# New durations in the table from which a kernel's planner orders every engine: an RWKV scan and two feed-forward layers on one Trainium2 core

## The chip, the core and the metric

The kernel runs on one core of a Trainium2 chip. The core has five engines with an instruction queue each: TensorE (PE, matmuls), VectorE (DVE), ScalarE (ACT), GpSimd (POOL) and SyncE (SP, which here issues all transfers from and to HBM). The metric is the device time of one launch in microseconds (us), lower is better; "the time" is the median of several runs.

## What is computed

Cut to what matters, the reference is:

```python
for t in range(S):                                  # 4 batches, 8 heads, 768 steps, width 48
    cur = einsum('bhd,bhe->bhde', u * kt, vt)
    y[:, :, t] = einsum('bhd,bhde->bhe', rt, state + cur)
    state = wt[..., None] * state + einsum('bhd,bhe->bhde', kt, vt)
x = y as (3072 tokens, 384)
h = x @ w_in;  x = (max(h, 0) + alpha * min(h, 0)) @ w_out      # 384 -> 2048 -> 384
h = x @ w_in2; out = (h * clip(h + 3, 0, 6) / 6) @ w_out2
```

The inputs and the result are float32.

## The kernel before

**Attention units.** The scan is cut into 48 units, each a quarter of the heads (two heads, 112 partitions) over 256 steps. Four units with the same steps are a third. A unit n loads its k, r and decays (`un`, 337 KB), runs two scans of the decays on DVE (lines 386 and 402, into `tg`), multiplies k and r by them (`kr`, line 423, DVE or POOL), and then goes through PE three times: scores and a transpose (`A`, lines 477 and 484), the state update (`kv`, lines 516 and 520, after ACT copied `kT`), and the output (`y`, lines 588 to 599). In between DVE puts the masked scores into `X` (lines 494 and 499) and updates `Y`, and ACT builds the diagonal `X` (458) and the states `sbd` (538). The result of a unit is split into a high part (ACT, 635) and a rest (DVE, 641). For units 0, 1 and 2 of a third these go straight into `xt`, the input of the first layer; for unit 3 they go into `x3`, which six small transfers (line 651) spread over `xt`. Each third also needs two loads of 128 tokens (`rk`, 384 KB), two multiplications of each (line 332, DVE or POOL) and a sum (`p`, line 339), and one load of v.

**Layers.** A layer runs 6 token blocks of 512 tokens by 16 slices of the hidden width: 96 slots, 192 in both layers. A slot is nine matmuls of 128x512 for `h` and nine for the three accumulators `acc` (three passes each, high and low parts), and between them `q` (ACT), `pg` (DVE, 808 or 812), `g` high (ACT, 818) and `g` low (DVE or POOL, 821). Slot s has `h`s, `q`s, `pg`s, `g`s. Before a slice is used for the first time, its two weights (384 KB each, `wraw`) are decoded: line 95 on ACT, lines 98 and 103 on DVE, 738 on ACT, 742 on DVE or POOL. `wraw0_f_0` is the first layer's weight of slice f into h, `wraw0_f_1` the one out of it.

**What sets the order.** The class `Plan` simulates the five engines with a list of operations, each with the engines that may run it, a duration for each of them in us, and a due time. At each step it takes the engine that can start soonest, and on it the ready operation with the earliest due time; an operation that DVE or POOL may run goes to whichever takes it first. Operations marked `pair` on DVE and all of POOL never overlap in this simulation. The sequence that comes out is the order in which every engine's instructions are written; at run time each engine works through its own list in that order, waiting where an input is not there. Fillers (line 682, `warm`, matmuls of 128x256 with no use for the result) are put on PE wherever the simulation finds it free before the first slot, and dropped after. A load on SP is planned with 1.12 us for 384 KB (1.0 for a unit) plus 2 us:

```python
            d = o["where"][e] * (2 if e == "PE" and t < self.COLD else 1)
            o["eng"], o["start"], o["end"] = e, t, t + d
            ...
            if e == "SP":
                o["end"] = t + d + 2.0
```

A load also waits for its buffer: there are three for `un`, two for `rk` and two for v. A weight of the first layer has a place of its own, so its load waits for nothing but its turn on SP.

Of the kernel before, what the change touches and what calls it, by code (L numbers as in the profile page):

```python
# [229 lines left out]
def fast_path(es, tc, unit, tok, vch, ub, w1, w2, alpha, out, flag, alp, x2d):  # L230
# [11 lines left out]
    plan = Plan()  # L242
# [50 lines left out]
    o_alpha = plan.op({"SP": 0.5}, -20.0, lambda e: nc.sync.dma_start(alp, alpha))  # L293
# [8 lines left out]
    Ylast, Yop = {}, {}  # L302
# [8 lines left out]
    def add_third(t):  # L311
# [9 lines left out]
        reds = []  # L321
        for c in range(2):
# [28 lines left out]
            reds.append(plan.op({"DVE": 0.47}, due + 4.5 + c, red, [o], new=[pb], use=[rb]))  # L351
        p_op[t] = reds, pb

    def add_unit(n):
# [46 lines left out]
        def scan_g(e):  # L401
# [8 lines left out]
        gb = plan.buf("gfirst", 2)  # L410
        o_t = plan.op({"DVE": 0.34}, d - 3.7, scan_t, [o_load], new=[tgb], use=[ub_], pair=True)
        o_f = plan.op({"DVE": 0.07}, d - 2.4, floor, [o_t], use=[tgb])
        o_d1 = plan.op({"DVE": 0.08}, d - 2, recip, [o_f], new=[gb])
        o_g = plan.op(
            {"DVE": 0.34}, d - 1.5, scan_g, [o_d1], use=[tgb, ub_, gb], pair=True
        )
# [12 lines left out]
        if early:  # L429
            o_kr = [  # L430
                plan.op(
                    {"DVE": 0.35, "POOL": 0.69}, d - 1, lambda e, i=i: scaled(e, slice(i, i + 1)),
                    [(o_t, o_g)[i]], new=[krb], use=[ub_, tgb], pair=True,
                )
                for i in range(2)
            ]
# [22 lines left out]

        o_x = plan.op({"ACT": 1.18}, d - 1, diag, reds, new=[xb], use=[pb])  # L460

# [66 lines left out]
        else:  # L528
            o_kv = plan.op({"PE": 0.1 + 0.13 * nkv}, d + 0.4, kv, kv_after, use=kv_use)
        o_tri = plan.op({"DVE": 0.61}, d - 1.5, triangle, [o_kv, o_x], use=abufs + [xb])  # L530

# [72 lines left out]
        def add_output(due=d + 2, more=0.0, then=None, after=(), use=()):  # L604
# [38 lines left out]
            fresh = [xt_buf[j]] + ([x3b] if x3b else [])  # L643
            o_hi = plan.op({"ACT": 0.36}, d + 2.5, hi_, [o_pc], new=fresh, use=[yb2])
            o_lo = plan.op({"DVE": 0.35}, d + 2.5, lo_, [o_hi], new=fresh, use=[yb2])
            ops += [o_hi, o_lo]
# [43 lines left out]
    def add_range(key, due, after=None, use=(), raw=None, behind=()):  # L690
# [78 lines left out]
    def add_slot(m, j, f):  # L769
# [9 lines left out]
        def h_(e):  # L779
# [44 lines left out]

        o_q = plan.op({"ACT": 0.58}, s + 1.1, pq, [o_h, o_alpha], new=[qb], use=[hb])
        o_g = plan.op({"DVE": 0.62}, s + 0.8, gate, [o_q], new=[pb], use=[qb, hb])
        o_1 = plan.op({"ACT": 0.52}, s + 1.0, ghi, [o_g], new=[gb], use=[pb])
        o_2 = plan.op({"POOL": 1.23, "DVE": 0.61}, s + 1.2, glo, [o_1], use=[pb, gb], pair=True)

# [366 lines left out]
```

## Time and profile before

| | us |
|---|---|
| time, median of 3 runs (944.39 to 947.23) | 945.42 |
| the profiled execution, its time | 945.74 |
| the profiled execution, its span | 944.0 |
| PE busy (share of the span) | 920.3 (97%) |
| DVE busy | 556.3 (59%) |
| ACT busy | 530.9 (56%) |
| POOL busy | 132.3 (14%) |

The span is the time from the first to the last instruction in one profiled execution; its own time is 1.7 us longer. Busy time is the time in which at least one instruction of the engine ran. The average over the whole span mixes a start, in which attention units and weights are prepared, with a long stretch in which only the slots and their units run.

### The profile page before, as it was taken

The page shows a single profiled execution, that of the slowest core. Times are in us where ns is not written, and L with a number is a line of the kernel's source. Part 1 is how long each engine was busy: PE and PEld are TensorE (multiplying, and loading weights), DVE is VectorE, ACT ScalarE, POOL GpSimd, SP SyncE. Part 2 cuts the span into 40 slices and gives each one's busy share as a digit, 9 for nine tenths or more (in the row PEclk, how much of TensorE's full clock was granted, in tenths as well). Part 3 has the DMA queues.
Part 4 walks back from the last instruction along what each step waited for, and adds up shares of the span by engine and source line. Part 5 has one row for each costly group of instructions (what it writes and reads, how often), then busy time and mean ns, then how long its engine had stood idle before and what let it go on. Part 6 is the DMA issues. An engine that isn't in the chain of part 4 may idle for free.

```text
span 944.0 us, 13745 instructions
## 1 busy us (share of the span) xinstructions
PE 920.3 (97%) x4914; PEld 743.2 (79%) x4914; DVE 556.3 (59%) x1087; ACT 530.9 (56%) x1266; POOL 132.3 (14%) x132
## 2 busy tenths in 40 slices
PE   7899989999999999999999999999999999999996
PEld 5677767878888788878888888888888888888885
DVE  8999997465655645564369886353353443443432
ACT  5998776565656655665378876363353453443331
POOL 4333234021121201100011130000000000000000
PEclk9999999999999999999999999999999999999998
DMA  8888214122312310110056530060140320500001
GB/s 250 256 268 283 81 52 145 55 79 70 107 64 57 109 55 31 58 64 7 9 186 197 175 111 1 1 200 1 54 147 1 123 79 1 172 30 1 34 1 38
DMA packets 36750, 86.20 MB, mean 91 GB/s; under 512 B 5056, under 2 KB 7488, under 8 KB 36672
## 3 DMA queue, kind: packets, MB, share of 16 engines
q1 hardware_dynamic: 36672, 85.22, 28.8%
q8 instruction: 41, 0.67, 0.3%
q14 instruction: 37, 0.30, 0.1%
HBM read 73.41 MB, written 9.44 MB: 88 GB/s over the span
## 4 chain that ended last, share of the span: by engine, by line
PE 82%; DVE 1%; DMA 0%; POOL 0%; issue 0%; POOLq 0%; DVEq 0%
PE acc L765 13%; PE acc L767 13%; PE acc L766 13%; PE h L765 12%; PE h L767 12%; PE h L766 12%; PE A L477 2%; PE y L595 1%; PE y L588 1%; PE A L484 1%; DMA rk<-in_tok 0%; PE y L599 0%; PE A L516 0%; POOL rk L332 0%; PE A L520 0%; DVE rk L332 0%
## 5 line engine op out<-in xcount | busy, mean ns | idle before, releaser
L765 PE MATMUL acc<-g,w 128*128 128x512 f32 x576 | 228.9, 397 | 0.0
L767 PE MATMUL acc<-g,w 128*128 128x512 f32 x576 | 224.6, 390 | 0.0
L766 PE MATMUL acc<-g,w 128*128 128x512 f32 x576 | 224.5, 390 | 0.0
L818 ACT ACTIVATE g<-pg 128x512 fp32r<-128x512 f32 x192 | 120.6, 628 | 137.7 <-PE acc L767 126.8
L821 DVE TENSOR_TENSOR g<-pg,g 128x512 fp32r<-128x512 f32 x176 | 121.7, 691 | 124.8 <-ACT g L818 124.7
L765 PEld LDWEIGHTS acc<-g,w 128*128 128x128 f32 x576 | 108.1, 188 | 23.4 <-issue 0.4
L767 PEld LDWEIGHTS acc<-g,w 128*128 128x128 f32 x576 | 108.1, 188 | 22.8
L766 PEld LDWEIGHTS acc<-g,w 128*128 128x128 f32 x576 | 108.2, 188 | 21.6 <-DVE g L821 0.3
L812 DVE SCALAR_TENSOR_TENSOR pg<-q,h 128x512 f32<-128x512 f32 x96 | 65.9, 686 | 98.6 <-ACT q L803 98.4
L808 DVE SCALAR_TENSOR_TENSOR pg<-h,q 128x512 f32<-128x512 f32 x96 | 66.1, 688 | 96.4 <-ACT q L801 96.3
L803 ACT ACTIVATE q<-h,three 128x512 f32<-128x512 f32 x96 | 65.8, 685 | 100.5 <-PE h L767 100.3
L765 PE MATMUL h<-xt,w 128*128 128x512 f32 x288 | 116.3, 404 | 1.2 <-ACT w L738 1.1
L767 PE MATMUL h<-xt,w 128*128 128x512 f32 x288 | 113.0, 392 | 0.9 <-POOL w L742 0.7
L766 PE MATMUL h<-xt,w 128*128 128x512 f32 x288 | 112.3, 390 | 0.0
L765 PE MATMUL h<-x,w 128*128 128x512 f32 x288 | 112.0, 389 | 0.0
L766 PE MATMUL h<-x,w 128*128 128x512 f32 x288 | 112.0, 389 | 0.0
L767 PE MATMUL h<-x,w 128*128 128x512 f32 x288 | 112.0, 389 | 0.0
L801 ACT ACTIVATE q<-h,nal 128x512 f32<-128x512 f32 x96 | 65.6, 684 | 73.6 <-PE h L767 71.7
L423 POOL TENSOR_TENSOR kr<-un,tg 112x512 f32<-112x512 f32 (+1 forms) x43 | 43.6, 1016 | 225.5 <-PE y L588 207.3
L765 PEld LDWEIGHTS h<-xt,w 128*128 128x128 f32 x288 | 54.9, 191 | 13.3 <-ACT w L738 2.2
L767 PEld LDWEIGHTS h<-xt,w 128*128 128x128 f32 x288 | 54.0, 188 | 14.1 <-DVE w L742 1.4
L766 PEld LDWEIGHTS h<-x,w 128*128 128x128 f32 x288 | 54.1, 188 | 11.3
(93 smaller groups left out, 1262.7 us busy)
## 6 DMA issues: line engine op xcount, KB each, us to landing
wraw<-in_w SPq DMA_DIRECT2D x64, 384.0 KB, 3.7
un<-in_unit SPq DMA_DIRECT2D x48, 337.3 KB, 3.2
raw<-in_w SPq DMA_DIRECT2D x32, 384.0 KB, 3.9
rk<-in_tok SPq DMA_DIRECT2D x24, 384.0 KB, 4.0
v<-in_vch SPq DMA_DIRECT2D x12, 384.0 KB, 3.1
x2d<-st SPq DMA_DIRECT2D x18, 256.0 KB, 2.1
x2r<-x2d SPq DMA_DIRECT2D x18, 256.0 KB, 4.6
out<-st SPq DMA_DIRECT2D x18, 256.0 KB, 3.5
```

The source lines that it names most:

```text
L423: eng[e].tensor_tensor(out=u["kr"][:, i].rearrange("p a (c s) -> p a c s", c=2), in0=u["in"][:, 0 : 2 * TH].rearrange("p (a c s) -> p a c ...
L477: nc.tensor.matmul(A[h][:, cs], kr[r0 : r0 + D, 0, cs], kr[r0 : r0 + D, 1, cs], start=True, stop=True,)
L484: nc.tensor.transpose(T[:, c, :], kr[:, 0, c * C : (c + 1) * C], ident[0:PR, 0:PR])
L765: nc.tensor.matmul(ps, whi, xhi, start=start, stop=False, skip_group_check=True)
L766: nc.tensor.matmul(ps, whi, xlo, start=False, stop=False, skip_group_check=True)
L767: nc.tensor.matmul(ps, wlo, xhi, start=False, stop=stop, skip_group_check=True)
L801: nc.scalar.activation(q, k["h"], AF.Relu, scale=nal[:, f : f + 1])
L803: nc.scalar.activation(q, k["h"], AF.Relu, bias=three)
L808: nc.vector.scalar_tensor_tensor(out=p, in0=k["h"], scalar=0.0, in1=k["q"], op0=ALU.max, op1=ALU.subtract)
L812: nc.vector.scalar_tensor_tensor(out=p, in0=k["q"], scalar=6.0, in1=k["h"], op0=ALU.min, op1=ALU.mult)
L818: nc.scalar.activation(k["g"][:, 0], k["p"], AF.Copy)
L821: eng[e].tensor_tensor(out=k["g"][:, 1], in0=k["p"], in1=k["g"][:, 0].bitcast(F32), op=ALU.subtract)
```

## The change

Most of the durations that the planner's list gives to operations on PE, DVE, ACT and POOL are replaced. Nearly all grow: on DVE the scans go from 0.34 to 0.69 each, a 384-wide operation from 0.47 to 0.55, `pg` from 0.62 to 0.69; on ACT the diagonal from 1.18 to 1.56, the states from 0.45 to 0.66, `g` high from 0.52 to 0.63; on PE `h` from 1.945 to 2.04 and an accumulator's three matmuls from 0.648 to 0.68. On POOL `rk` and the weights' low part go from 0.96 to 1.06 and 1.05, `g` low from 1.23 to 1.33, and `kr` of 112x512 from 1.25 down to 1.08. The loads' durations, the due times and everything else stay. No instruction is computed differently; what moves is the order on each engine, and the choice between DVE and POOL. A few lines of the diff:

```diff
-                    {"POOL": 0.96, "DVE": 0.47}, due + 2 + c, lambda e, b=b, m=mul: m(e, b=b),
+                    {"POOL": 1.06, "DVE": 0.55}, due + 2 + c, lambda e, b=b, m=mul: m(e, b=b),
...
-        o_t = plan.op({"DVE": 0.34}, d - 3.7, scan_t, [o_load], new=[tgb], use=[ub_], pair=True)
+        o_t = plan.op({"DVE": 0.69}, d - 3.7, scan_t, [o_load], new=[tgb], use=[ub_], pair=True)
...
-                    {"DVE": 0.61, "POOL": 1.25}, d - 1, lambda e: scaled(e, slice(0, 2)), [o_g],
+                    {"DVE": 0.7, "POOL": 1.08}, d - 1, lambda e: scaled(e, slice(0, 2)), [o_g],
```

What the new order holds, counted: PE has 206 fillers instead of 128, all ahead of the first slot. Up to the low part of the last weight of the first layer POOL has 57 instructions of the plan instead of 43 (`rk` 18 for 11, `kr` of 112x512 10 for 3, `kr` of 112x256 8 for 11, weights 13 for 10, `g` 7 and 7, one other). Up to `pg16` DVE has 3 `rk`, 7 `kr` of 112x512 and 3 weight operations (742) fewer, and 3 `kr` of 112x256 and 2 sums (339) more. From slot 20 on, PE's order differs only in where a unit's `A` stands between the three accumulators of a slot.

Three places, before and after. In the rows the number right behind a name is that of the unit, the load or the weight (`un6`, `rk7`, `wraw0_2_0`); the last number only tells buffers apart.

SP before, from unit 5's load to unit 7's, issued some 17 to 26 us into the span:

```order
L368 DMA un5_324<-in_unit 112x771
L729 DMA wraw0_1_0_343<-in_w1 128x384
L368 DMA un6_366<-in_unit 112x771
L328 DMA rk4_386<-in_tok 128x768
L729 DMA wraw0_2_0_409<-in_w1 128x384
L328 DMA rk5_429<-in_tok 128x768
L368 DMA un7_459<-in_unit 112x771
```

SP after the change, from unit 5's load to `rk4`:

```order
L368 DMA un5_321<-in_unit 112x771
L729 DMA wraw0_2_0_339<-in_w1 128x384
L729 DMA wraw0_0_1_366<-in_w1 128x384
L729 DMA wraw0_3_0_377<-in_w1 128x384
L729 DMA wraw0_1_1_399<-in_w1 128x384
L729 DMA wraw0_4_0_418<-in_w1 128x384
L368 DMA un6_439<-in_unit 112x771
L328 DMA rk4_458<-in_tok 128x768
```

Five weights stand between units 5 and 6 where one stood (`wraw0_1_0` comes ahead of `un5` now).

SP before, from `rk6` to the six transfers of `x3` of the second third (one row for all six), which the first slot needs:

```order
L328 DMA rk6_670<-in_tok 128x768
L729 DMA wraw0_4_0_688<-in_w1 128x384
L368 DMA un11_709<-in_unit 112x771
L729 DMA wraw0_2_1_731<-in_w1 128x384
L328 DMA rk7_745<-in_tok 128x768
L368 DMA un12_767<-in_unit 112x771
L651 DMA xt0_294<-x3_1_749 16x2x256 x6
```

SP after the change, the same stretch:

```order
L328 DMA rk6_633<-in_tok 128x768
L729 DMA wraw0_5_0_651<-in_w1 128x384
L729 DMA wraw0_3_1_676<-in_w1 128x384
L729 DMA wraw0_6_0_687<-in_w1 128x384
L368 DMA un10_706<-in_unit 112x771
L729 DMA wraw0_4_1_730<-in_w1 128x384
L328 DMA rk7_744<-in_tok 128x768
L729 DMA wraw0_7_0_762<-in_w1 128x384
L368 DMA un11_784<-in_unit 112x771
L729 DMA wraw0_5_1_800<-in_w1 128x384
L317 DMA v3_813<-in_vch 128x768
L729 DMA wraw0_8_0_832<-in_w1 128x384
L651 DMA xt0_334<-x3_1_825 16x2x256 x6
```

Between `rk6` and `rk7` stand four weights instead of two, and five loads instead of one between `rk7` and the six transfers.

DVE before, up to the rest of unit 7 (`x3_1`), some 43 to 47 us into the span:

```order
L641 TENSOR_TENSOR xt0_294<-y6_659,xt0_294 112x256
L402 SCALAR_TENSOR_TENSOR tg1_112<-un9_591,gfirst1_110 112x258
L332 TENSOR_TENSOR rk6_670<-rk6_670 128x384
L423 TENSOR_TENSOR kr9_737<-un9_591,tg1_112 112x512
L742 TENSOR_TENSOR w0_1_0_734<-wb0_1_0_407,w0_1_0_734 128x384
L562 SCALAR_TENSOR_TENSOR Y8_0_753<-Y4_1_520,tg0_111,A8_696 112x48
L499 COPY_PREDICATED X8_632<-mask_91,A8_696 128x512
L641 TENSOR_TENSOR x3_1_749<-y7_724,x3_1_749 112x256
```

DVE after the change, up to the same instruction:

```order
L641 TENSOR_TENSOR xt0_334<-y6_720,xt0_334 112x256
L399 RECIPROCAL gfirst1_110<-fall_99 112x2
L103 SCALAR_TENSOR_TENSOR wb0_0_0_483<-wraw0_0_0_267,wb0_0_0_483 128x384
L402 SCALAR_TENSOR_TENSOR tg1_112<-un9_621,gfirst1_110 112x258
L332 TENSOR_TENSOR rk7_744<-rk7_744 128x384
L562 SCALAR_TENSOR_TENSOR Y8_0_818<-Y4_1_563,tg0_111,A8_778 112x48
L499 COPY_PREDICATED X8_734<-mask_91,A8_778 128x512
L641 TENSOR_TENSOR x3_1_825<-y7_790,x3_1_825 112x256
```

`kr9` and `rk6` are POOL's now, the first weight (`wb0_0_0`) is decoded here instead of earlier, and a multiplication of `rk7` stands ahead of `X8` and `x3_1`.

## Rows read from the trace of the kernel before

**Rows 1.** The page: busy time of each engine, its share of the span, its instructions; and the shares of the chain of work that ended last.

```profile
PE 920.3 (97%) x4914; PEld 743.2 (79%) x4914; DVE 556.3 (59%) x1087; ACT 530.9 (56%) x1266; POOL 132.3 (14%) x132
...
PE 82%; DVE 1%; DMA 0%; POOL 0%; issue 0%; POOLq 0%; DVEq 0%
```

**Rows 2.** Busy time of each engine in stretches of 50 us (from and to, in us from the span's start; length; busy us and instructions of PE, weight loads, DVE, ACT, POOL; granted clock; DMA share; GB/s).

```profile
0.00:50.00 50.00, 40.53 (x389) 29.89 (x390) 46.02 (x123) 38.11 (x130) 19.49 (x34) 0.97 0.82 249
50.00:100.00 50.00, 48.41 (x295) 36.26 (x294) 49.93 (x104) 43.44 (x118) 17.40 (x15) 1.00 0.83 264
100.00:150.00 50.00, 46.56 (x278) 35.24 (x277) 45.79 (x95) 36.80 (x95) 15.81 (x14) 1.00 0.23 69
...
200.00:250.00 50.00, 50.00 (x300) 40.05 (x299) 29.88 (x63) 29.02 (x77) 8.62 (x8) 1.00 0.25 79
```

**Rows 3.** Whom PE waited for: us in total, times, longest us.

```profile
PE A L477 <- DVE kr L423: 4.9, 6, 1.4
...
PE h L765 <- ACT w L738: 1.1, 3, 0.4
```

**Rows 4.** PE in order of time, 49 to 53.5 us (start, us, line, tile, count, in brackets idle time before it): the last fillers, y of unit 9, A of unit 10, the first matmul of the first slot.

```profile
49.47 1.70 PE L682 MATMUL warm<-ident 128*128 128x256 bf16 x14
51.37 0.66 PE L588 MATMUL y<-kr,sbd 112*112 112x128 f32 x4 [0.20 <-DVE xt L641]
...
52.53 0.71 PE L477 MATMUL A<-kr 48*128 48x128 f32 x8
...
53.26 0.48 PE L765 MATMUL h<-xt,w 128*128 128x512 f32 x1
```

**Rows 5.** Three stretches of 10 us, columns as in Rows 2.

```profile
10.00:20.00 10.00, 8.39 (x81) 6.06 (x77) 9.27 (x25) 7.89 (x28) 4.17 (x6) 0.85 0.95 271
...
30.00:40.00 10.00, 8.73 (x96) 6.87 (x95) 9.97 (x28) 9.46 (x34) 2.48 (x3) 1.00 0.57 177
...
60.00:70.00 10.00, 9.19 (x54) 6.91 (x54) 10.00 (x22) 9.23 (x24) 2.57 (x2) 1.00 1.04 322
```

**Rows 6.** SP in order of time: when `wraw0_1_0`, `un6`, `rk7` and the six transfers of `x3_1` were issued.

```profile
17.59 0.43 SPq L729 DMA_DIRECT2D wraw<-in_w  x1
20.61 0.33 SPq L368 DMA_DIRECT2D un<-in_unit  x1
...
43.23 0.38 SPq L328 DMA_DIRECT2D rk<-in_tok  x1
...
47.42 4.66 SPq L651 DMA_DIRECT2D xt<-x  x6
```

**Rows 7.** The view of transfers, asked for three of these issues alone (`wraw0_1_0`, `un6`, `rk7`): the last column is us from issue to landing.

```profile
wraw<-in_w SPq DMA_DIRECT2D x1, 384.0 KB, 5.8
...
un<-in_unit SPq DMA_DIRECT2D x1, 337.3 KB, 4.1
...
rk<-in_tok SPq DMA_DIRECT2D x1, 384.0 KB, 6.0
```

**Rows 8.** DVE in order of time: the first scan of unit 6, and a `kr` of 112x256.

```profile
26.47 1.33 DVE L386 TENSOR_TENSOR_SCAN tg<-un,restart 112x258 f32<-112x258 f32 x1
...
28.96 0.40 DVE L423 TENSOR_TENSOR kr<-un,tg 112x256 f32<-112x256 f32 x1
29.28 0.69 DVE L402 TENSOR_TENSOR_SCAN tg<-un,gfirst 112x258 f32<-112x258 f32 x1
```

**Rows 9.** DVE in order of time, 44.6 to 47 us, up to the rest of unit 7 (`x3_1`), and a sum (339) with what follows it.

```profile
44.67 0.53 DVE L332 TENSOR_TENSOR rk<-rk 128x384 f32<-128x384 f32 x1
45.12 0.68 DVE L423 TENSOR_TENSOR kr<-un,tg 112x512 f32<-112x512 f32 x1
45.72 0.55 DVE L742 TENSOR_TENSOR w<-wb,w 128x384 fp32r<-128x384 f32 x1
46.19 0.25 DVE L562 SCALAR_TENSOR_TENSOR Y<-Y,tg,A 112x48 f32<-112x48 f32 x1
...
46.99 0.40 DVE L641 TENSOR_TENSOR x<-y,x 112x256 fp32r<-112x256 f32 x1
...
51.15 0.53 DVE L339 TENSOR_REDUCE p<-rk 128x8 f32<-128x384 f32 x1
51.61 0.91 DVE L386 TENSOR_TENSOR_SCAN tg<-un,restart 112x258 f32<-112x258 f32 x1
```

**Rows 10.** Two places where a POOL instruction and a DVE instruction with two inputs lie at the same time, in order of time on each engine.

```profile
40.57 1.15 POOL L742 TENSOR_TENSOR w<-wb,w 128x384 fp32r<-128x384 f32 x1 [5.60 <-ACT w L738]
...
40.78 1.49 DVE L423 TENSOR_TENSOR kr<-un,tg 112x512 f32<-112x512 f32 x1
...
55.12 1.27 POOL L423 TENSOR_TENSOR kr<-un,tg 112x512 f32<-112x512 f32 x1 [1.29 <-issue]
...
55.35 1.45 DVE L742 TENSOR_TENSOR w<-wb,w 128x384 fp32r<-128x384 f32 x1
```

**Rows 11.** Three stretches behind the start of the first slot, columns as in Rows 2.

```profile
53.30:100.00 46.70, 45.31 (x264) 33.94 (x265) 46.63 (x97) 40.40 (x108) 14.10 (x13) 1.00 0.87 278
100.00:147.00 47.00, 43.56 (x259) 33.02 (x258) 42.89 (x87) 34.01 (x87) 14.75 (x14) 1.00 0.21 60
147.00:160.00 13.00, 12.71 (x75) 9.90 (x74) 10.29 (x24) 8.95 (x25) 6.36 (x7) 1.00 0.66 209
```

More of the change, by code (lines that the diff above doesn't have):

```diff
@@ L347, in add_third @@
                 o = plan.op(
-                    {"POOL": 0.96, "DVE": 0.47}, due + 2 + c, lambda e, b=b, m=mul: m(e, b=b),
+                    {"POOL": 1.06, "DVE": 0.55}, due + 2 + c, lambda e, b=b, m=mul: m(e, b=b),
                     [o] + after, use=[rb], pair=True,
                 )
-            reds.append(plan.op({"DVE": 0.47}, due + 4.5 + c, red, [o], new=[pb], use=[rb]))
+            reds.append(plan.op({"DVE": 0.54}, due + 4.5 + c, red, [o], new=[pb], use=[rb]))
         p_op[t] = reds, pb
@@ L410, in add_unit @@
         gb = plan.buf("gfirst", 2)
-        o_t = plan.op({"DVE": 0.34}, d - 3.7, scan_t, [o_load], new=[tgb], use=[ub_], pair=True)
-        o_f = plan.op({"DVE": 0.07}, d - 2.4, floor, [o_t], use=[tgb])
-        o_d1 = plan.op({"DVE": 0.08}, d - 2, recip, [o_f], new=[gb])
+        o_t = plan.op({"DVE": 0.69}, d - 3.7, scan_t, [o_load], new=[tgb], use=[ub_], pair=True)
+        o_f = plan.op({"DVE": 0.17}, d - 2.4, floor, [o_t], use=[tgb])
+        o_d1 = plan.op({"DVE": 0.16}, d - 2, recip, [o_f], new=[gb])
         o_g = plan.op(
-            {"DVE": 0.34}, d - 1.5, scan_g, [o_d1], use=[tgb, ub_, gb], pair=True
+            {"DVE": 0.69}, d - 1.5, scan_g, [o_d1], use=[tgb, ub_, gb], pair=True
         )
@@ L431, in add_unit @@
                 plan.op(
-                    {"DVE": 0.35, "POOL": 0.69}, d - 1, lambda e, i=i: scaled(e, slice(i, i + 1)),
+                    {"DVE": 0.43, "POOL": 0.72}, d - 1, lambda e, i=i: scaled(e, slice(i, i + 1)),
                     [(o_t, o_g)[i]], new=[krb], use=[ub_, tgb], pair=True,
@@ L449, in check @@
             )
-        plan.op({"ACT": 0.42}, d + 1, check, [o_load], use=[ub_])
+        plan.op({"ACT": 0.61}, d + 1, check, [o_load], use=[ub_])
         def diag(e):
@@ L458, in diag @@
                 nc.scalar.activation(X[:, i], ident, AF.Copy, scale=pp[:, i : i + 1])
-        o_x = plan.op({"ACT": 1.18}, d - 1, diag, reds, new=[xb], use=[pb])
+        o_x = plan.op({"ACT": 1.56}, d - 1, diag, reds, new=[xb], use=[pb])
         alt = early and n % 2 == 1
@@ L529, in add_unit @@
             o_kv = plan.op({"PE": 0.1 + 0.13 * nkv}, d + 0.4, kv, kv_after, use=kv_use)
-        o_tri = plan.op({"DVE": 0.61}, d - 1.5, triangle, [o_kv, o_x], use=abufs + [xb])
+        o_tri = plan.op({"DVE": 0.73}, d - 1.5, triangle, [o_kv, o_x], use=abufs + [xb])
         sb = [plan.buf("sbd", 4), plan.buf("sbd", 4)]
@@ L643, in add_output @@
             fresh = [xt_buf[j]] + ([x3b] if x3b else [])
-            o_hi = plan.op({"ACT": 0.36}, d + 2.5, hi_, [o_pc], new=fresh, use=[yb2])
-            o_lo = plan.op({"DVE": 0.35}, d + 2.5, lo_, [o_hi], new=fresh, use=[yb2])
+            o_hi = plan.op({"ACT": 0.57}, d + 2.5, hi_, [o_pc], new=fresh, use=[yb2])
+            o_lo = plan.op({"DVE": 0.41}, d + 2.5, lo_, [o_hi], new=fresh, use=[yb2])
             ops += [o_hi, o_lo]
@@ L712, in check @@
             )
-        o_v = plan.op({"DVE": 0.27}, due - 1.5, upper, [after], new=[vb], use=use, pair=True)
-        plan.op({"ACT": 0.6}, due + 1, check, [o_v], use=[vb])
+        o_v = plan.op({"DVE": 0.37}, due - 1.5, upper, [after], new=[vb], use=use, pair=True)
+        plan.op({"ACT": 0.8}, due + 1, check, [o_v], use=[vb])
         return o_v
@@ L747, in add_weight @@
         o_l = plan.op({"SP": 1.12}, due - 4, load, new=[wb])
-        o = plan.op({"ACT": 0.42}, due - 0.2, rest, [o_l], new=[ab, bb], use=[wb])
+        o = plan.op({"ACT": 0.63}, due - 0.2, rest, [o_l], new=[ab, bb], use=[wb])
         for i in (1, 2):
             o = plan.op(
-                {"DVE": 0.47}, due - 2, lambda e, i=i: k["steps"][i](), [o], use=[wb, ab, bb],
+                {"DVE": 0.55}, due - 2, lambda e, i=i: k["steps"][i](), [o], use=[wb, ab, bb],
                 pair=True,
@@ L754, in add_weight @@
         read = [add_range(key, due, o_l, [wb], lambda: k["raw"])] if m else []
-        o = plan.op({"ACT": 0.42}, due - 2.5, hi, [o] + read, use=[wb, bb])
+        o = plan.op({"ACT": 0.52}, due - 2.5, hi, [o] + read, use=[wb, bb])
         w_ops[key] = plan.op(
-            {"POOL": 0.96, "DVE": 0.47}, due - 1, lo, [o], use=[bb, wb], pair=True
+            {"POOL": 1.05, "DVE": 0.55}, due - 1, lo, [o], use=[bb, wb], pair=True
         )
@@ L823, in glo @@
             )
[L825 to L828, printed above, removed]
+        o_q = plan.op({"ACT": 0.69}, s + 1.1, pq, [o_h, o_alpha], new=[qb], use=[hb])
+        o_g = plan.op({"DVE": 0.69}, s + 0.8, gate, [o_q], new=[pb], use=[qb, hb])
+        o_1 = plan.op({"ACT": 0.63}, s + 1.0, ghi, [o_g], new=[gb], use=[pb])
+        o_2 = plan.op({"POOL": 1.33, "DVE": 0.7}, s + 1.2, glo, [o_1], use=[pb, gb], pair=True)
         if f == 0:
```

8 lines of the change are left out of this document (4 added, 4 removed).

## The prediction

> **What bounds the kernel now.** I read the page's shares first. PE is busy for 97% of the span and holds 82% of the chain that ended last [rows 1], but that is an average, so the stretches come next. From 200 us on PE is busy in every microsecond and DVE in 60% of them; in the first 150 us it is DVE that is full (46.0, 49.9 and 45.8 of 50 us), while PE has gaps [rows 2]. So there are two regimes: a start paced by DVE, and a long stretch in which PE alone counts. From slot 20 on PE's matmuls keep their order but for the place of each unit's A, and nobody waits there. The change can only gain or lose in the start: the time is PE's fixed work plus what PE loses before it runs full.
>
> What it loses lies in two parts. Before the first slot, whose first matmul starts at 53.26, it is mostly waiting or running fillers [rows 4]. Behind it, from 53.3 to 160 us, it idles 1.39 + 3.44 + 0.29 = 5.1 us [rows 11], at `kr` from DVE and at weights just in time [rows 3]. DVE is busy 46.63 of 46.7 us up to 100 and 42.89 of 47 up to 147, so it has 4.1 us of air there.
>
> **The change on DVE and POOL.** New durations alone cost nothing; only the order counts. Up to `pg16` (146 us before) DVE has 13 operations fewer and 5 more. I price them by the spacing of neighbours that wait for nothing: `rk` 45.12 - 44.67 = 0.45, `kr` of 112x512 0.60, a weight's low part 0.47 [rows 9], `kr` of 112x256 0.32 [rows 8], a sum 0.46 [rows 9]. So 3 x 0.45 + 7 x 0.60 + 3 x 0.47 - 3 x 0.32 - 2 x 0.46 = **5.1 us less work on DVE**.
>
> This isn't free, since POOL gets 14 instructions more. At 40.78 a `kr` on DVE takes 1.49 us beside a POOL instruction that started at 40.57, and 0.68 where POOL is silent; a weight's low part takes 1.45 beside POOL against 0.55 [rows 9, 10]. A collision thus costs DVE 0.8 to 0.9 us, but not each POOL instruction collides. From 53.3 to 147 DVE is busy 89.5 us [rows 11]; the operations that stand there add up, by such spacings, to some 79.4 (an estimate), so 10.1 us are collisions, over 13 + 14 = 27 POOL instructions: 0.37 each. The bounds for 14 more are 0 (the new order puts POOL beside operations that don't collide) and 14 x 0.9 = 12.6; I take 14 x 0.37 = **5.2 us**, the mean of this very stretch. That eats the gain. The Trainium skill (SBUF — State Buffer, section Who interferes with whom) states it as a rule: a VectorE operation with two SBUF inputs and a GpSimd operation that reads SBUF exclude each other, and the later one waits for the whole of the other. The rows agree in kind; were every one of the 14 to block DVE in full, the sum would be 12.6 instead of 5.2.
>
> **The loads.** The diff leaves SP's durations alone, so with slower engines the planner finds SP ahead of them and fills it with weights, which wait for no buffer. In the trace the transfers are full at that time: 271 GB/s at a share of 0.95, later 322 at full share [rows 5]. For 384 KB (393 KB in thousands) that is 1.45 to 1.22 us; the plan counts 1.12.
>
> *Unit 6.* Before, `wraw0_1_0` lands at 17.59 + 5.8 = 23.4 and `un6` at 20.61 + 4.1 = 24.7, back to back [rows 6, 7]; its scan starts at 26.47 [rows 8]. Now five more weights stand ahead of `un6`, so it lands at 24.7 + 5 x (1.22 to 1.45) = 30.8 to 32.0. DVE reaches the scan with one `rk`, one weight operation and one reciprocal less, and one `kr` and one `xt` more, some 0.3 us earlier, at 26.1. In its place stands **a wait of 4.7 to 5.9 us, 5.3 in the middle**. Behind the scan on DVE stand the scans of units 5 to 7 and `X4`; ACT's check of the same load stands ahead of the diagonal of unit 4. Both engines stop, and PE, which waits for `kT4`, runs fillers.
>
> *`rk7`.* The rest of unit 7 (`x3_1`) ran at 46.99 [rows 9]. Ahead of it DVE has one operation each of lines 98, 103 and 742 less, three `rk` and two large `kr` less, three small `kr` more: 0.47 x 3 + 0.45 x 3 + 0.60 x 2 - 0.32 x 3 = 3.0 us. With the wait: 46.99 - 3.0 + 5.3 = 49.3. But the multiplication of `rk7` now stands 0.45 + 0.8 us ahead of it, so it is due at 48.0. Before, `rk7` landed at 43.23 + 6.0 = 49.2 [rows 6, 7]. Now some 14 loads of 384 KB stand from `rk4` to `rk7` behind `un6`: 31.4 + 14 x (1.22 to 1.45) = 48.5 to 51.7. **Another wait of 0.5 to 3.7 us; I take 2.1**, and `x3_1` comes at 51.4. The 30th to 40th us of before, where the share was 0.57 [rows 5], show that the queue had air there which the weights now use up.
>
> *The first slot.* From `x3_1` to the first matmul it took 53.26 - 46.99 = 6.3 us, through six transfers issued from 47.42 on over 4.66 us [rows 4, 6, 9]. Now `rk7` and five more loads (4.9 of 384 KB, 6 to 7 us) go ahead of them in the queue, which ends at 50.1 + 6.5 = 56.6, so the transfers aren't late by it: 51.4 + 6.3 = **57.7, 4.4 us later**. And A of unit 10, which took 0.73 us ahead of the first slot [rows 4], stands behind it now: PE is 5.1 us behind.
>
> *Fillers.* 78 more at 1.70 / 14 = 0.12 us [rows 4] are 9.5 us of PE. I cost them at nothing, since they lie in the waits for units 0 to 9; where such a wait is gone, the 15 to 17 in a row cost up to 2 us.
>
> **The sum.** On DVE up to `pg16`: -5.1 + 5.2 + 5.3 + 2.1 = +7.5 us, of which the 4.1 us of air can take back as much as they hold: +3.4 to +7.5. On PE: +5.1, of which its 5.1 us of idle time can be won back: 0 to +5.1. The later of the two sets the end. I take **+4.0**, near the lower end, since a wait of 5 us gives PE and POOL time to run ahead. The profiled execution took 945.74, the median is 945.42, so 949.7 on its scale is **949.4** as a median.
>
> **Rivals.**
>
> *Faster.* The loads arrive in time, the collisions don't grow, and the 5.1 us come through, bounded by the idle time of PE. For it: the new durations are near the measured ones, so POOL and DVE can be laid side by side better. Against it: five weights ahead of `un6` are in the order, and the rows price each at 1.2 us or more. With a wait of 1 us and 0.1 us for each POOL instruction: -5.1 + 1.4 + 1.0 = -2.7, 942.7. It decides at `un6`: landed by 27 us, this is the case. The Trainium skill (DMA: Bandwidth & Descriptors, section Specifications) gives about 358 GB/s from HBM for a core, an estimated 1.10 us for 384 KB; by it `un6` would still land only at 30.2, 0.6 us ahead of my earliest, so it doesn't carry this case; the stretches at full share show 271 to 322.
>
> *No difference.* The wait for `un6` comes, the one for `rk7` doesn't, and each POOL instruction costs 0.2: -5.1 + 2.8 + 5.3 = +3.0, and three quarters of the air on DVE take it back to nothing: 945.4, up to 948.
>
> *Much slower.* The queue stays full at 1.45 us, POOL costs 0.6: -5.1 + 8.4 + 5.9 + 3.7 = +12.9, less 4.1: 954.2. The first slot would then start near 60.
>
> **How the numbers follow.** 0.3% (2.8 us) is about what a measurement of this kernel can tell from no change. My own case (948.3 to 952) has 0.43, much slower 0.11, no difference 0.27, faster 0.19. Slower by over 0.3% is then 0.54, within 0.27, faster 0.19. The range leaves out half of the faster case (below 942.7) and a tenth of the slow end: 942.7 to 954.5. The likeliest case's own range is 948.3 to 952.
>
> **What would show it.** In the profile after: DVE idle or ACT idle for 4 us and more at the scan or the check of unit 6, released by the transfer of `un`; a wait of DVE for `rk` near 48 to 52; the first `h` at 56 to 59; DVE's time in line 423 down and POOL's busy time up by some 14 us up to 150; PE full from 200 us on as before. Wrong I am if `un6` lands before 27 us, if the waits are there but PE's idle time behind 53 us shrinks by all of it, or if PE has gaps after 200 us, of which I expect none.

## The result and the profile after

The change makes the kernel slower: 956.68 us as the median of 5 runs (952.28 to 957.62) against 945.42 (944.39 to 947.23), a ratio of 1.0108 (95% interval 1.0080 to 1.0137). The direction was forecast, the size was not: 949.4 was predicted, with 954.5 as the upper end. The profiled execution took 957.62 us with a span of 955.8, 11.8 more than before.

Busy time and its shares in the profile after, to be read beside [rows 1]:

```profile
PE 929.9 (97%) x4992; PEld 751.6 (79%) x4992; DVE 567.8 (59%) x1080; ACT 534.7 (56%) x1265; POOL 143.8 (15%) x140
```

The same stretches as in [rows 2], after (length; busy us of PE, weight loads, DVE, ACT, POOL; granted clock; DMA share; GB/s):

```profile
0.00:50.00 50.00, 43.02 (x408) 34.14 (x410) 40.82 (x107) 31.85 (x107) 19.09 (x34) 0.93 0.90 262
50.00:100.00 50.00, 43.59 (x295) 31.47 (x292) 45.97 (x86) 40.43 (x118) 22.62 (x18) 1.00 0.79 252
100.00:150.00 50.00, 46.18 (x260) 34.16 (x259) 48.25 (x95) 37.80 (x91) 22.25 (x18) 1.00 0.21 64
200.00:250.00 50.00, 50.00 (x308) 40.14 (x307) 29.04 (x62) 29.08 (x77) 9.65 (x9) 1.00 0.26 79
```

The loss is made in the start, as forecast: from 200 us on PE is full. DVE does 5.2 us less in the first 50 us (40.82 for 46.02), so it waited there; POOL does 11.3 us more up to 150 us (64.0 for 52.7). The clock is new: 0.93 in the first stretch, where before had 0.97.

DVE's longer waits up to 53 us, in order of time, without the loads of units 0 and 1 and the first `rk` ahead of 12 us (Y is the state, `A` the scores that it needs, `tg` of 30.89 the first scan of unit 6, `rk` of 52.98 the multiplication of `rk7`):

```profile
15.29 0.21 DVE L560 COPY Y<-A 112x48 f32<-112x48 f32 x1 [1.03 <-PE A L520]
...
19.90 0.21 DVE L560 COPY Y<-A 112x48 f32<-112x48 f32 x1 [0.63 <-PE A L520]
...
24.00 0.21 DVE L560 COPY Y<-A 112x48 f32<-112x48 f32 x1 [1.16 <-PE A L520]
...
26.92 0.21 DVE L560 COPY Y<-A 112x48 f32<-112x48 f32 x1 [1.00 <-PE A L520]
...
30.89 0.69 DVE L386 TENSOR_TENSOR_SCAN tg<-un,restart 112x258 f32<-112x258 f32 x1
...
52.98 0.56 DVE L332 TENSOR_TENSOR rk<-rk 128x384 f32<-128x384 f32 x1 [2.96 <-DMA rk<-in_tok]
```

The forecast wait at unit 6's scan is not there: its load was issued at 26.57 and took 3.3 us, and DVE came at 30.89, 4.4 us later than before [rows 8]. SP in order of time, the load itself, the DMA share from 26 to 28 us (columns as above), what SP waited for ahead of it (us in total, times, longest), and the instruction on ACT that ended this wait:

```profile
18.30 2.33 SPq L729 DMA_DIRECT2D wraw<-in_w  x5
26.57 0.33 SPq L368 DMA_DIRECT2D un<-in_unit  x1
...
un<-in_unit SPq DMA_DIRECT2D x1, 337.3 KB, 3.3
...
26.00:28.00 2.00, 2.00 (x28) 1.83 (x28) 1.08 (x5) 1.93 (x9) 0.00 (x0) 1.00 0.70 219
...
SPq L368 <- ACT junk L446: 3.6, 1, 3.6
...
25.99 0.42 ACT L446 ACTIVATE junk<-un 112x259 bf16<-112x259 f32 x1
```

The five weights ahead of `un6` were all issued by 20.6 us. SP then waited for the buffer of unit 3, whose check ACT ran at 25.99 only (at 20.04 before). When the load went out, the transfers were no longer full (0.70), so in this kernel it was the buffer rather than the weights that set its landing at 29.8.

DVE was late already, through four short waits for PE. The first of them begins on ACT:

```profile
11.18 0.42 ACT L446 ACTIVATE junk<-un 112x259 bf16<-112x259 f32 x1 [5.33 <-DMA un<-in_unit]
...
12.77 0.42 ACT L446 ACTIVATE junk<-un 112x259 bf16<-112x259 f32 x1 [1.07 <-DMA un<-in_unit]
...
14.36 0.33 ACT L509 ACTIVATE kT<-A 128x224 f32<-128x224 f32 x1
```

`kT` of unit 0 now stands behind the checks of units 1 and 2, which wait for their loads. On PE (same columns) the state update of unit 0 waits 2.87 us for it, and soon after it the matmuls are slow (the last row is the first matmul of the first slot):

```profile
14.74 0.26 PE L516 MATMUL A<-v,kT 128*64 128x48 f32 x1 [2.87 <-ACT kT L509]
...
15.76 1.23 PE L477 MATMUL A<-kr 48*128 48x128 f32 x8
...
59.98 0.48 PE L765 MATMUL h<-xt,w 128*128 128x512 f32 x1
```

The eight matmuls of `A` take 1.23 us instead of the 0.71 of [rows 4]: the granted clock is at its lower level (1.2 of 2.4 GHz) in this stretch, after PE had idled. Two windows of the kernel after show it, 0.78 and 0.87; before had 0.85 in the first of them [rows 5] and 1.00 in the second:

```profile
10.00:20.00 10.00, 7.13 (x63) 5.72 (x62) 7.07 (x16) 6.27 (x22) 4.24 (x6) 0.78 1.04 272
20.00:30.00 10.00, 10.00 (x102) 8.04 (x103) 7.64 (x24) 7.40 (x27) 3.52 (x6) 0.87 0.93 292
```

**Where DVE's time went.** DVE paces the start, so I split its time up to `pg16` in every kernel. Each form of operation has an undisturbed spacing (a scan 0.60, an `rk` 0.45, a `kr` of 112x512 0.60, a part of a weight 0.46 or 0.47, `pg` and `g` 0.60, and so on, as in [rows 8, 9]); their sum is the *work*, time in which DVE runs nothing is *idle*, and the rest, what operations take beyond their spacing, is the *excess*. All three are counted from the first scan (3.9 us before, 4.1 after). An example of excess, in the kernel after: a `kr` on POOL, in order of time,

```profile
61.73 1.17 POOL L423 TENSOR_TENSOR kr<-un,tg 112x512 f32<-112x512 f32 x1 [1.25 <-DVE tg L402]
```

and on DVE a part of a weight that starts beside it and takes 1.44 us instead of 0.54, holding up what follows:

```profile
61.87 1.44 DVE L98 SCALAR_TENSOR_TENSOR wb<-wraw,wa 128x384 int32<-128x384 int32 x1
```

Another, on POOL and on DVE, with an operation that takes 0.17 us where POOL is silent and reads one tile only:

```profile
68.17 1.01 POOL L742 TENSOR_TENSOR w<-wb,w 128x384 fp32r<-128x384 f32 x1 [2.33 <-ACT w L738]
...
68.30 0.91 DVE L394 TENSOR_SCALAR fall<-tg 112x2 f32<-112x2 f32 x1
```

| up to `pg16`, us | starts at | idle | work | excess | POOL instructions | DVE operations held by over 0.3 us |
|---|---|---|---|---|---|---|
| before | 142.8 | 6.4 | 118.2 | 14.2 | 45 | 17 |
| after | 156.1 | 13.1 | 113.1 | 25.8 | 58 | 30 |
| difference | +13.3 | +6.7 | -5.1 | +11.5 | +13 | +13 |

So 5.1 us of work were saved, as forecast, 6.7 us of waits were added, and 11.5 us of excess. (Up to the rest of unit 7, at 46.99 before and 54.25 after, idle is 2.3 and 10.3.) Every one of the held operations lies beside an elementwise instruction of POOL, and they lose 0.7 to 0.8 us each on average; six of the 17 and nine of the 30 are `fall`. Some of the expectations below quote an excess of 16.2 and 26.7 us and an idle time of 12.1: they were written with an earlier split, which put less down to work.

### The profile page after: what moved, and what is told of

It reads as the page before. It is cut to its first block, busy times and chain, and to the rows that moved or that the text cites. A ratio compares the mean times of both kernels' runs of the same rounds, so it can differ in the third digit from the quotient of the medians.

```text
span 955.8 us, 13903 instructions
## 1 busy us (share of the span) xinstructions
PE 929.9 (97%) x4992; PEld 751.6 (79%) x4992; DVE 567.8 (59%) x1080; ACT 534.7 (56%) x1265; POOL 143.8 (15%) x140
## 4 chain that ended last, share of the span: by engine, by line
PE 84%; DVE 1%; issue 0%; DVEq 0%
PE acc L765 14%; PE acc L767 13%; PE acc L766 13%; PE h L765 13%; PE h L767 13%; PE h L766 13%; PE A L477 2%; PE y L595 2%; PE y L588 1%; PE A L484 1%; PE A L516 0%; PE y L599 0%; DVE wb L98 0%; PE A L520 0%; DVE wb L103 0%
## 5 line engine op out<-in xcount | busy, mean ns | idle before, releaser
L423 POOL TENSOR_TENSOR kr<-un,tg 112x512 f32<-112x512 f32 (+1 forms) x47 | 49.1, 1045 | 257.4 <-PE y L588 218.4
L767 PEld LDWEIGHTS h<-xt,w 128*128 128x128 f32 x288 | 54.0, 188 | 13.4 <-DVE w L742 2.0
L765 PEld LDWEIGHTS h<-x,w 128*128 128x128 f32 x288 | 54.1, 188 | 11.2
L766 PEld LDWEIGHTS h<-x,w 128*128 128x128 f32 x288 | 54.1, 188 | 11.2
```

The lines of the kernel that those rows point to most:

```text
L423: eng[e].tensor_tensor(out=u["kr"][:, i].rearrange("p a (c s) -> p a c s", c=2), in0=u["in"][:, 0 : 2 * TH].rearrange("p (a c s) -> p a c ...
L765: nc.tensor.matmul(ps, whi, xhi, start=start, stop=False, skip_group_check=True)
L766: nc.tensor.matmul(ps, whi, xlo, start=False, stop=False, skip_group_check=True)
L767: nc.tensor.matmul(ps, wlo, xhi, start=False, stop=stop, skip_group_check=True)
```

## The experiments

Three theories stood at first; others came with the results and are told where they enter. Theory 1: the table is now right for four engines and wrong for the loads, and the two errors had offset each other. Theory 2: POOL's additional instructions block DVE. Theory 3: a few single waits carry it all. Ratios are to the kernel before, timed beside it on the same chip, with their 95% intervals.

### The loads' durations measured too

```diff
-            o = plan.op({"SP": 1.12}, due + c, load_rk, new=[rb])
+            o = plan.op({"SP": 1.4}, due + c, load_rk, new=[rb])
...
-        o_load = plan.op({"SP": 1.0}, d - 4 if n else -50.0, load, new=[ub_])
+        o_load = plan.op({"SP": 1.25}, d - 4 if n else -50.0, load, new=[ub_])
```

> The changed kernel with the durations of the loads set to what the traces show as well: 1.40 us for 384 KB instead of 1.12, 1.25 instead of 1.00 for a unit, 0.75 instead of 0.60 for u (393 KB in thousands at the 271 to 322 GB/s of full stretches are 1.22 to 1.45 us). Theory 1 (the table is now right for four engines and wrong for the loads, so the planner puts instructions where their data has not come yet): most of the loss goes, 944 to 949 us, the first slot at 51 to 55 instead of 60, DVE idle up to the rest of unit 7 down from 12.1 to under 8 us. Theory 2 (the instructions that the new durations move to POOL block DVE): POOL's share stays, so 952 to 957 us. Theory 3 (two single waits, kT of unit 0 and rk7, carry the loss): no firm number; better only if both go.

955.89 us, 1.0088 (1.0064 to 1.0111): the loss stays, theory 1 falls as a whole. Its first half came true. The rest of unit 7 ran at 50.8 instead of 54.3 and the first slot at 56.4 instead of 60.0. The gain went behind the first slot, and the profile's windows name the place:

```profile
62.00:64.00 2.00, 1.26 (x14) 0.84 (x13) 2.00 (x6) 1.90 (x6) 0.00 (x0) 1.00 1.03 395
64.00:66.00 2.00, 1.14 (x8) 0.96 (x8) 2.00 (x5) 1.85 (x5) 0.00 (x0) 0.67 1.03 272
66.00:68.00 2.00, 2.00 (x7) 1.60 (x6) 2.00 (x5) 1.96 (x6) 0.00 (x0) 0.50 1.03 281
68.00:70.00 2.00, 2.00 (x6) 1.61 (x5) 1.95 (x5) 0.51 (x2) 0.00 (x0) 0.50 1.03 399
70.00:72.00 2.00, 2.00 (x14) 1.44 (x14) 0.00 (x0) 0.01 (x1) 0.00 (x0) 0.62 1.03 399
```

PE is idle for 1.6 us between 62 and 66, the granted clock falls to 0.50 and stays there into the last window, where DVE and ACT have nothing to do: DVE waits 3.96 us for PE, up to 73.9.

### That clock taken away

Fillers are allowed up to the first accumulator, 30 more, all behind the first slot; no other instruction moves.

```diff
-        o_h["starts"] = True
...
+            o_o["starts"] = True
```

> The changed kernel with the measured durations of the loads and with the fillers allowed up to the first accumulator instead of up to the first slot: 30 more of them, 27 between A of unit 10 and A of unit 11, where PE was nearly idle from 62.6 to 64.9 us and the granted clock was 0.50 from 65 to 71 us. If this clock cost the gain of the measured loads (theory 7): the clock stays at 1.00 there, nine matmuls of h that took 3.9 us take 2.1, DVE's wait of 3.96 us behind them shrinks, and the time falls by 3 to 5 us, to 951 to 953. If not, the fillers only delay: within 1.5 us of the 955.9 without them.

952.14 us, 1.0068 (1.0045 to 1.0092), against 955.89, 1.0088 (1.0064 to 1.0111), without them. The medians are 3.8 us apart, which is in the range that was given, but the kernel before, timed beside each, was 1.4 us faster here: by the ratios it is some 1.9 us, and the intervals overlap. Two of the same windows:

```profile
64.00:66.00 2.00, 2.00 (x21) 1.59 (x20) 0.65 (x3) 0.43 (x2) 0.00 (x0) 1.00 1.04 277
66.00:68.00 2.00, 2.00 (x17) 1.52 (x16) 2.00 (x5) 1.96 (x6) 0.00 (x0) 1.00 1.02 373
```

The clock stays at 1.00, and DVE's longest wait there is 1.35 us instead of 3.96; `pg16` starts at 155.1 instead of 156.0. So the lower clock and the wait that it causes are shown, but that they cost the time of the whole kernel 3 to 5 us isn't: a gain in time is not clear of noise. The excess on DVE is 23.3 us without and 23.6 with the fillers.

### Single waits

`kT` of unit 0 goes ahead of the two checks on ACT:

```diff
+        at = {o["tag"]: i for i, o in enumerate(seq) if "tag" in o}
+        seq.insert(at["check", 1], seq.pop(at["kT", 0]))
```

> The changed kernel with one instruction moved on one engine: ACT copies kT of unit 0 ahead of its checks of units 1 and 2 instead of behind them; all other queues keep their order. In the changed kernel kT of unit 0 ends at 14.7 us, held up by the loads of units 1 and 2. Theory 3 (single waits): DVE's wait of 1.03 us ahead of Y of unit 0 goes, and TensorE is idle 2.9 us less, so the end comes 1 to 3 us earlier. Theories 1 and 2: units 1 to 3 still come late or DVE is still blocked later, so at most 0.5 us.

954.87 us, 1.0080 (1.0057 to 1.0102); the interval overlaps that of the changed kernel, so no gain can be told. The profile shows why. `kT` is done 4.4 us earlier, DVE comes to unit 6's scan early, and there stands the wait that I had forecast:

```profile
31.39 0.70 DVE L386 TENSOR_TENSOR_SCAN tg<-un,restart 112x258 f32<-112x258 f32 x1 [3.07 <-DMA un<-in_unit]
```

Its buffer came free earlier, so its load was issued at 23.84, while the transfers were full, and took 7.5 us behind the five weights. The rest of unit 7 ran at 54.1, as without the move.

`rk7` goes ahead of the four weights between `rk6` and `rk7`:

```diff
+        late = [o for o in seq[a:b] if o.get("tag", " ")[0] == "w"]
+        seq[a : b + 1] = [o for o in seq[a : b + 1] if o not in late] + late
```

> The changed kernel with the load of rk7 issued ahead of the four weights that stand between rk6 and rk7, which go right behind it; no other queue changes. In the changed kernel DVE waits 2.96 us for rk7 at 50 to 53 us. Theory 3 (single waits): that wait goes and the first slot starts about 3 us earlier, the time falls by 2 to 3 us. Theory 1: the queue is full in that stretch, the four weights only land later by what rk7 gains, and the wait comes back elsewhere: within 1.5 us of the changed kernel, either way. Theory 2: within 0.5 us.

956.48 us, 1.0102 (1.0076 to 1.0128): nothing. The wait for `rk7` goes and the rest of unit 7 runs at 48.10; behind the first slot a wait of 3.17 us takes its place:

```profile
48.10 0.41 DVE L642 TENSOR_TENSOR x<-y,x 112x256 fp32r<-112x256 f32 x1
...
63.04 0.27 DVE L563 SCALAR_TENSOR_TENSOR Y<-Y,tg,A 112x48 f32<-112x48 f32 x1 [3.17 <-ACT w L739]
```

The row names a weight on ACT, but this operation also needs `A`, whose matmuls PE ran at 62.6 only, behind nine of `h`, most of them at the lower clock (columns as before). The clock fell here as in the first run:

```profile
58.00:60.00 2.00, 2.00 (x6) 1.51 (x5) 1.87 (x4) 0.00 (x0) 0.19 (x1) 0.55 0.86 304
60.00:62.00 2.00, 2.00 (x12) 1.19 (x10) 0.00 (x0) 0.00 (x0) 0.00 (x0) 0.60 0.98 321
```

Both moves at once, and the five weights behind `un6` as well:

```diff
+        for first, last in ((("un", 5), ("un", 6)), (("rk", 6), ("rk", 7))):
+            a, b = place()[first], place()[last]
+            late = [o for o in seq[a:b] if o.get("tag", " ")[0] == "w"]
+            seq[a : b + 1] = [o for o in seq[a : b + 1] if o not in late] + late
```

> The changed kernel with three local moves: kT of unit 0 ahead of the checks of units 1 and 2 on ACT, the five weights between un5 and un6 behind un6, the four weights between rk6 and rk7 behind rk7; DVE, POOL and PE keep their order. Alone, the first move brought up a wait of 3.07 us at the scan of unit 6 in place of the one it removed, and the third brought the rest of unit 7 to 48.1 us but a wait of 3.17 us for a weight behind the first slot. Theory 6 (the waits of the start are stacked and the collisions between DVE and POOL stay): the rest of unit 7 at 46 to 49 us, but collisions of 25 us and later weights keep the time at 951 to 956 us. Theory 3 in its full form (the waits at the loads carry the loss): 945 to 949 us.

965.25 us, 1.0193 (1.0132 to 1.0254): by the medians some 8 us worse than leaving all alone, though its runs spread from 957 to 969 us. Both theories missed it. `un6` waits for its buffer until 25.12 us; the weights that had stood ahead of it used that time, and now everything on SP stands behind it. The DMA share from 20 to 30 us falls to 0.43 (first row), PE's clock to 0.68 (last row):

```profile
20.00:30.00 10.00, 10.00 (x102) 8.03 (x100) 7.23 (x22) 7.21 (x28) 2.53 (x4) 0.88 0.43 138
30.00:40.00 10.00, 6.38 (x65) 4.94 (x63) 4.35 (x13) 6.49 (x23) 2.43 (x3) 0.98 0.82 262
40.00:50.00 10.00, 9.33 (x74) 7.10 (x74) 6.24 (x20) 4.36 (x14) 4.24 (x5) 0.68 0.68 201
```

The wait moves on to unit 7's scan, on DVE in order of time:

```profile
38.74 0.70 DVE L388 TENSOR_TENSOR_SCAN tg<-un,restart 112x258 f32<-112x258 f32 x1 [4.31 <-DMA un<-in_unit]
```

Theory 3 is out: no move of a single wait, nor all of them together, brought a gain clear of noise, and behind each wait that went another came up.

### POOL and DVE

The 43 instructions of the start whose engine the change swaps go back to their old engine, in the new order:

```diff
+            if o["id"] in SWAP:
+                o["eng"] = "DVE" if o["eng"] == "POOL" else "POOL"
```

> The changed kernel's sequence, but each of the 43 instructions of the start (up to 165 us in the plan) for which the choice between DVE and POOL differs goes back to the engine that it had before; SP, ACT and PE keep the changed order. Theory 2 (POOL's 14 additional instructions block DVE by 0.8 us each): DVE gets some 4 us more work and 10 us fewer collisions, so 949 to 951 us. Theory 1 (the order against the loads): the idle time of DVE in the start stays, the time is 953 to 958 us.

961.87 us, 1.0139 (1.0105 to 1.0174): no better, and above what either theory gave. DVE's work rises by 6.9 us to 120.1, but the excess falls by 4.1 us alone, to 21.7, with 45 POOL instructions as before; 26 operations are held, where the old order had 17. So it isn't their number alone; theory 2 falls in the form "14 more instructions, 0.8 us each".

That the excess is POOL's doing at all was tested by taking POOL away, in both orders:

```diff
+            if o["eng"] == "POOL" and o["flex"] and o["start"] < 165:
+                o["eng"] = "DVE"
```

> The changed kernel's sequence with the 60 multiplications, products and low parts that POOL takes up to 165 us of the plan given to DVE, in their places. They are some 29 us of work for DVE (60 by 0.48). Theory 6 (the 26.7 us by which DVE's operations take longer than their undisturbed spacing up to pg16 are blocked by POOL): that excess falls below 9 us, so the time moves little, 953 to 963 us. If the excess has another cause, it stays and the 29 us come on top: 970 us and more.

> The same done to the kernel before: 49 instructions from POOL to DVE, some 23 us of work, against an excess of 16.2 us. Theory 6: the excess falls below 9 us and the time rises by 4 to 14 us, to 950 to 960; then POOL is worth about that much in the old order and next to nothing in the new one. If the excess has another cause: 965 us and more.

955.10 us, 1.0096 (1.0067 to 1.0124), and 951.49 us, 1.0062 (1.0037 to 1.0086). The excess up to `pg16` is 2.2 and 1.4 us, with work of 140.2 and 138.0, and no operation is held by over 0.3 us: the excess was POOL's, as theory 6 has it. DVE alone does all of it in the same time as DVE and POOL together in the new order (1.0096 for 1.0108), while in the old order POOL is worth 0.6%, some 5.8 us. And the two orders without POOL, on one chip, are 3.6 us apart, not 11; the intervals of these two overlap, so the 3.6 is known to a few us only. By the medians two thirds of the loss are thus POOL's help, which the old order got and the new one doesn't.

### Any other table?

One engine's numbers alone (DVE's, then ACT's, as in the change), a constant that says nothing of durations, and the loads' measured durations in the old table:

```diff
-        o_t = plan.op({"DVE": 0.34}, d - 3.7, scan_t, [o_load], new=[tgb], use=[ub_], pair=True)
+        o_t = plan.op({"DVE": 0.69}, d - 3.7, scan_t, [o_load], new=[tgb], use=[ub_], pair=True)
...
-        o_x = plan.op({"ACT": 1.18}, d - 1, diag, reds, new=[xb], use=[pb])
+        o_x = plan.op({"ACT": 1.56}, d - 1, diag, reds, new=[xb], use=[pb])
...
-    SPARE = 0.46
+    SPARE = 0.2
```

> The kernel before with only the durations of DVE's operations new. Its order has what the changed one has: seven weights ahead of un6 (two before), the checks of units 1 and 2 ahead of kT of unit 0, 55 instructions of POOL up to pg16 (44 before). Theory 5 (the numbers of DVE carry the loss): 953 to 958 us, DVE idle up to the rest of unit 7 near 10 us. Theory 4 (the old table is one set of numbers tuned together, and any departure from it loses some us): slower too, 949 to 962 us; this run alone doesn't tell them apart.

> The kernel before with only the durations of ACT's operations new. POOL has 48 instructions up to pg16, near the 44 of before; four weights stand ahead of un6. Theory 5 (DVE's numbers carry the loss): 945 to 949 us. Theory 4 (any departure loses): 950 to 958 us.

> The kernel before with one constant of the planner changed that says nothing about durations: the lead in due time that an operation for DVE or POOL gives up on DVE, 0.2 instead of 0.46. The order up to un6 stays nearly the same; POOL has 49 instructions up to pg16 instead of 44. Theory 4 (the old constants are tuned together): slower by 2 to 6 us, 947 to 952. Theory 5: within 2 us of before, 944 to 948.

> The kernel before with only the durations of the loads set to the measured ones (1.40, 1.25 and 0.75 us), everything else old. One weight stands ahead of un6 instead of two. If wrong numbers of the loads cost before anything (what is left of theory 1): 940 to 945 us. Theory 4 (tuned together): 946 to 952 us. Theory 5: within 2 us of before.

In this order: 960.10 us, 1.0132 (1.0105 to 1.0158); 963.18 us, 1.0172 (1.0144 to 1.0201); 953.83 us, 1.0077 (1.0053 to 1.0100); 951.83 us, 1.0044 (1.0029 to 1.0059). All lose against the kernel before. Theory 5 falls with ACT's numbers, which alone cost more than all numbers together. What the parts cost doesn't add up: each table is another order. DVE's numbers bring idle time of 26.4 us up to `pg16` and an excess of 16.4, ACT's 11.6 and 25.5, the constant 4.0 and 22.7, the loads 11.4 and 17.5: waits in one order, collisions in another.

This looked like theory 4: the old table as a tuned point which any departure leaves. Two departures in which all engines keep their old durations tested it:

```diff
-    LATENCY = 0.08
+    LATENCY = 0.2
...
-            o = plan.op({"SP": 1.12}, due + c, load_rk, new=[rb])
+            o = plan.op({"SP": 1.25}, due + c, load_rk, new=[rb])
```

> The kernel before with the loads at 1.25 us for 384 KB (1.112 for a unit, 0.669 for u) and the planner's hand-over time between engines at 0.2 us instead of 0.08; all durations of the engines old. POOL has 47 instructions up to pg16 (44 before). Theory 4 in its hard form (any departure from the old table loses): 949 to 955 us, as the loads alone did (951.8). Theory 8 (other orders as good as the old one exist, where loads and hand-overs are given more time and the collisions stay low): 940 to 946 us, the excess on DVE up to pg16 at most 18 us, the first slot at 50 to 55.

> The same with the loads at 1.30 us (1.157 and 0.696): a step of 4% in one number from the run beside it, in the size of what can be read wrong in a trace. POOL has 39 instructions up to pg16. Theory 8: within 3 us of the run beside it. Theory 4: 949 to 955 us, and more than 3 us from the run beside it, either way, since the order jumps.

942.21 us, 0.9943 (0.9920 to 0.9965), faster than both kernels, and 946.34 us, 0.9987 (0.9973 to 1.0002), no difference. The hard form of theory 4 falls: other good orders exist. But 4% in the loads' duration move the time by 4.1 us, more than the 3 us that theory 8 had allowed. The faster one is within theory 8 (first slot at 52.7). DVE's longest waits up to 142 us are short (us in total, times, longest), and PE is fuller than before from 60 to 165 us (102.87 us busy for 99.92). The waits, and the window:

```profile
DVE p L339 <- POOL rk L332: 1.5, 1, 1.5
DVE tg L386 <- DMA un<-in_unit: 1.3, 2, 1.0
```

```profile
60.00:165.00 105.00, 102.87 (x617) 80.02 (x616) 101.19 (x205) 81.91 (x213) 47.58 (x29) 1.00 0.52 160
```

Its idle time up to `pg16` is 2.9 us and its excess 13.7, with 47 POOL instructions and 16 operations held; the granted clock is 1.00 in every stretch of the start. Whether the loads' time or the hand-over time brings this wasn't taken apart, and why the changed order has more collisions than the old one, instruction by instruction, stays open as well: the runs show that it is the order, and not the number of POOL's instructions alone.

One more reading of the table belongs here. The plan keeps an engine busy for the whole duration, and the old numbers are close to the spacing of neighbours that wait for nothing: `rk` 0.47 for 0.45, a `kr` of 112x512 0.61 for 0.60 [rows 9]; on ACT the diagonal (four operations) 1.18, where in the kernel before the next operation starts 1.17 us after it:

```profile
11.30 1.26 ACT L458 ACTIVATE X<-ident,p 128x128 f32<-128x128 f32 x4
12.47 0.66 ACT L538 ACTIVATE sbd<-Y,tg 48x48 f32<-48x48 f32 x2
```

The new numbers (0.55, 0.70, and 1.56 for the four) are close to the lengths of the single instructions (0.53, 0.68, four of 0.39), which overlap their neighbours. So for most operations of DVE and ACT the new table counts too much, and only for some, as the scans (0.34 old, 0.69 new, spacing 0.60), is it nearer. A table of spacings was not run, so what this costs isn't shown.

## Why the prediction was wrong

*The direction and the place* were right: a start paced by DVE, no loss behind 200 us, waits at the loads.

*Collisions, "14 x 0.37 = 5.2 us, the mean of this very stretch": the term that failed.* The excess grew by 11.5 us, with 13 more operations held for 13 more POOL instructions. The mean was about sound for the old order (14.2 us over 45 instructions are 0.32), but it is a property of an order, not of an instruction: 0.44 in the new one, 0.48 with the old engines in the new order, 0.29 in the fast one (13.7 over 47). I took the mean of an order that has few collisions and carried it over to one that has many. The Trainium skill (SBUF — State Buffer, section Who interferes with whom) has the two exclude each other in full; by that rule, with every one of the 14 colliding, the term would have been 12.6 instead of 5.2, and the 11.5 measured are close to it.

*"-5.1 us less work on DVE"*: the operations were counted right, and by the same spacings the table gives 5.1 again. `pg16` started at 142.8 before, not at 146.

*The wait at unit 6, "4.7 to 5.9 us": it did not come, for two reasons on ACT.* I had DVE come to the scan at 26.1; it came at 30.9, held up by `kT` of unit 0 behind two checks and by PE at its lower clock. And `un6`, forecast to land at 30.8 to 32.0 behind five weights, landed at 29.8 because its buffer came free at 26.5, behind ACT's late check of unit 3. None of this was in the sum: I looked at DVE's and SP's queues up to unit 6, not at ACT's, and let PE's first 50 us go by as "waiting or running fillers", though [rows 5] had a clock of 0.85 in them. With `kT` moved the load came earlier into a full queue and the forecast wait appeared, 3.07 us, so the mechanism exists; it did not act in the kernel that was forecast. By luck the sizes agree: idle time up to the rest of unit 7 grew by 8.0 us, where 5.3 + 2.1 = 7.4 had been forecast.

*`rk7`, "I take 2.1":* 2.96, within the 0.5 to 3.7; DVE came 2.0 us later than forecast, and the load landed at 53.0, behind the 48.5 to 51.7. *The first slot at 57.7:* 59.98; from the rest of unit 7 it took 5.7 us for the 6.3 forecast.

*"I take +4.0, near the lower end": the second failure.* I let 3.5 of 7.5 us be taken back by air. Behind the rest of unit 7 DVE's idle time fell from 4.2 to 2.9 us only, and PE's behind the first slot rose: up to the first matmul of slot 21 it was 5.2 of 111.8 us before, 7.9 of 117.1 after; the first slot came 6.7 us later and slot 21 12.0. With the measured terms the sum on DVE is -5.1 + 11.5 + 8.0 - 1.3 = +13.1, against 13.3 measured at `pg16` and 11.8 at the end.

*The rivals.* Much slower (954.2, with 0.6 us for each POOL instruction and a first slot near 60) was nearest, and had 0.11. No difference and faster needed small waits or cheap collisions; neither was there.

## What to carry to other kernels

A list planner's table is a set of knobs: other numbers on some of its engines give another order, not a better one, and the time of an order can't be had by adding up what its parts cost. What an engine's queue spends on an operation is the spacing of neighbours, not the length of one instruction. Price a collision between two engines from the whole of the blocked instruction, not from the mean of an order that has few of them, and read every queue from the first microsecond, ACT's checks that free buffers and PE's clock included. When one wait is taken away, look for the next one behind it before counting the gain; where a small change of a table moves the time by 0.4% and more, as here, try many tables and time them.

## What had not been expected of the hardware

PE's clock at its lower level costs waits on DVE, which paces the start: 1.6 us of idle PE were followed by some 7 us at 0.50 and a wait of 3.96 us on DVE, and with 27 fillers in that gap the clock stayed at 1.00 and the wait was 1.35; in the run with `rk7` moved the lower clock stood in a wait of 3.17 us. And transfers reached 395 to 399 GB/s over 2 us, more than the 322 that [rows 5] have over 10 us and the prediction took as their best; over 10 us the kernel after has 394:

```profile
69.00:79.00 10.00, 9.54 (x54) 6.93 (x54) 9.48 (x17) 8.82 (x24) 6.32 (x6) 1.00 1.03 394
```

POOL's elementwise instructions held not only operations of DVE with two inputs: `fall`, with one, took 0.91 us for 0.17.
